# Weights' signs from ScalarE's parametric ReLU, and eight heads with split values in place of four

## The chip, the cores and the metric

The kernel runs on one core of a Trainium2 chip. The metric is the time of one execution on the device in microseconds (us), smaller is better; the time before is the median of three runs. A core has five engines that matter here: TensorE (PE in the profile; PEld is its weight load), VectorE (DVE), ScalarE (ACT), GpSimd (POOL) and SyncE (SP). Each runs its own instructions in the order in which they were queued, and waits for others by semaphores. POOL and SP here mostly start transfers between memory and the on-chip buffer.

## The reference

An attention in which a query sees only the keys in its own hash bucket (six sign bits of a projection), and then two feed-forward blocks without residuals:

```
mask   = q_bucket[:, :, :, None] == k_bucket[:, :, None, :]     # (2, 8, 768, 768)
scores = where(mask, q @ k.T / sqrt(64), -1e9)
x = softmax(scores) @ v                    # 16 heads; x is (1536, 512)
h = x @ w_in                               # 512 x 2048
x = (h * tanh(softplus(h))) @ w_out        # 2048 x 512
a = x @ w1;  b = x @ w2                    # 512 x 1024 each
out = ((a * b) @ w3) @ w_out2              # 1024 x 1024, 1024 x 512
```

The inputs q, k, v and proj are float32; the six weight matrices are float64 and reach the kernel as pairs of 32-bit words.

## The kernel before, in words

**Precision.** Most products run on PE in a fast reduced format (`FR` in the code, `fp32r` in the profile). Where that is not exact enough, a factor is split into a high part (a cast to `FR`) and a low part (the rest), and the product takes three or four fast passes. The other way is one product in full float32, which PE takes more slowly and which the profile shows as two instructions.

**Attention.** 16 heads, numbered u = 0 to 15, each of 768 rows in six tiles of 128. For each score tile: four matmuls on PE (L537), the row maximum on DVE (L546), the exponential on ACT (L549). Then each 128 x 128 piece of the exponentials is transposed on PE (L591, three to an operation), copied out of PSUM into a tile T by ACT or DVE (L415), and multiplied by the values: a head has six value steps, each over two blocks of keys (L620, function `values`). In most heads the value step is two float32 products with 64 columns each. In the heads of `FRV`, before u = 3 to 6, values are split: the copy casts T to `FR`, a DVE subtraction makes T's low part (L600), the values themselves are cast (`vh`, on ACT or DVE) and subtracted (`vl`, L449) once a head into one tile that holds both parts, and the step is four fast products with 128 columns. A Val of kind "v" in pool F4 holds the split values; its limit (`Val(F4, "v", 3, FR)`) says how many heads may have one at a time.

**Weights.** 36 chunks of 128 x 1024 float64 numbers are loaded by POOL (L668, 1 MB each) and turned into float32 by `decode`: ACT scales the high words, read as float32, so that their exponents fall where a shift by three bits makes them those of the result (step a, L652, a Copy with a scale); DVE shifts (step b, L655), puts in the low words' upper bits (step c, L658) and the sign bit of step a's result (step d, L661). Twelve chunks make the product w3 @ w_out2 during the first heads (L743 to L770). The other 24 are stored to memory, and loaded and split (L710 on ACT, L712 on DVE) when their matmuls come.

**Stages.** The 1536 rows are three blocks of 512. Block 0's feed-forward (L959, L975, L1070) is mixed with heads 8 to 15 on PE. Blocks 1 and 2 come after the attention, with products on quarter tiles that need seven multiplications for eight (L906, L1327, L1369).

**What sets the order.** Every operation is given to a planner, `Plan.op`, with the engines that may run it, a cost, and a due time; `Plan.run` lays them out engine by engine: at each turn it takes the engine that can start first, and of its ready operations the one due first. An operation with two engines (`EITHER`) goes to the one that can start it first. Buffers are given out in the same pass, and the instructions are then recorded in the order of planned starts. The numbers in `CFG` are due times (`prep`, `wp0`, `dec0`, `ff0`, `clk` and others) and buffer limits (`hl`, `F`), so a changed number or cost moves instructions all over the program. Gaps on PE in the first part are filled with products that nobody reads (L406).

Of the kernel before, what the change touches and what calls it, by code (L numbers as in the profile page):

```python
# [8 lines left out]
F32 = mybir.dt.float32  # L9
FR = mybir.dt.float32r  # L10
I32 = mybir.dt.int32
AF = mybir.ActivationFunctionType
ALU = mybir.AluOpType
# [6 lines left out]
LEAST = float(2.0 ** -126)  # L20
HUGE = float(2.0 ** 100)
TINY = float(2.0 ** -80)
SIGN = -(2 ** 31)

PASS = ((0, 0), (0, 1), (1, 0))

CFG = {
    "lag": 1.92,
    "prep": 11.76,
    "wp0": 16.6,  # L30
    "wp1": 42.29,
    "dec0": 39.06,
    "dec1": 124.72,
    "ff0": 55.14,
    "ff1": 118.67,
    "slack": 0.10,
    "k8": 12,
    "f4": 7,
    "hl": 3,
    "hl2": 6,  # L40
    "sl": 2,
    "lag2": 1,
    "lag3": 1,
    "hlk": 2,
    "ahead": 13.19,
    "clk": 190.46,
    "g2": 3,
    "F": 2,
    "cold": 8.0,
    "fill": 60.0,  # L50
    "tc": 0,
    "T": 8,
    "VP": 3,
    "fv0": 3,
    "fv1": 7,
}


# [36 lines left out]
class Plan:  # L95
# [87 lines left out]
    def run(self):  # L183
        todo = {e: [] for e in self.free}
        count = 0
        for u in self.pending:
            if u.left == 0:
                for e in u.alts:
                    todo[e].append(u)
        total = len(self.pending)  # L190
        self.pending = []
        order = []

        def grab_time(u):
            t = 0.0
            for v in u.vals:
                if v.pool is not None and v.slot is None:
                    p = v.pool
                    if p.kinds.get(v.kind, 0) >= v.lim or not p.free:
                        return None  # L200
                    t = max(t, min(p.free)[0])
            return t

        while count < total:
            best = None
            for e, cand in todo.items():
                s = None
                for u in cand:
                    if u.start is not None:
                        continue  # L210
                    t = max(u.ready, self.free[e])
                    if s is not None and t > s + 1e-9:
                        continue
                    g = grab_time(u)
                    if g is None:
                        continue
                    t = max(t, g)
                    if s is None or t < s:
                        s = t
                if s is not None and (best is None or s < best[0]):  # L220
                    best = (s, e)
            if best is None:
                left = [u for e in todo for u in todo[e] if u.start is None]
                raise RuntimeError("plan is stuck: " + ", ".join(f"{u.name}({u.due:.1f})" for u in left[:40]))
            s, e = best
            pick = None
            for u in todo[e]:
                if u.start is not None or max(u.ready, self.free[e]) > s + 1e-9:
                    continue
                if pick is not None and (u.due, u.idx) >= (pick.due, pick.idx):  # L230
                    continue
                g = grab_time(u)
                if g is None or g > s + 1e-9:
                    continue
                pick = u
            u = pick
            u.start, u.eng = s, e
            for v in u.vals:
                if v.pool is not None and v.slot is None:
                    p = v.pool  # L240
                    f = min(x for x in p.free)
                    p.free.remove(f)
                    v.slot = f[1]
                    v.since = s
                    p.kinds[v.kind] = p.kinds.get(v.kind, 0) + 1
            cost = u.alts[e] * (1.7 if e == "PE" and s < CFG["cold"] else 1.0)
            u.alts[e] = cost
            end = s + cost
            if u.grow:
                u.grow(end + 0.5)  # L250
            self.free[e] = end
            order.append(u)
            count += 1
            todo[e] = [x for x in todo[e] if x.start is None]
            for v in u.vals:
                if v.pool is not None and not v.pin and all(x.start is not None for x in v.users):
                    t = max(self.out_time(x, True, _ANY) for x in v.users)
                    v.pool.free.append((t, v.slot))
                    v.pool.spans.setdefault(v.slot, []).append((v.since, t))
                    v.pool.kinds[v.kind] -= 1  # L260
            for x, data in u.succ:
                x.ready = max(x.ready, self.out_time(u, data, x))
                x.left -= 1
                if x.left == 0:
                    for ee in x.alts:
                        todo[ee].append(x)
        order.sort(key=lambda u: (u.start, u.idx))
        if self.filler:
            self.fill(order)
            order.sort(key=lambda u: (u.start, u.idx))  # L270
        for u in order:
            u.fn(u.eng) if len(u.alts) > 1 else u.fn()
        return order
# [26 lines left out]
def kernel(  # L300
# [14 lines left out]
    nc = tc.nc  # L315
# [6 lines left out]
    NH = B * H  # L322
# [10 lines left out]
    P = Plan()  # L333
# [30 lines left out]
    F4 = anypool("f", CFG["f4"], 1024, const)  # L364
# [65 lines left out]
    def load_v(u, due, after=()):  # L430
# [11 lines left out]

        P.op("POOL", 1.3, total, r=[t], w=[m], due=u * C, name=f"vs{u}")
        if u in FRV:
            g = vs[u] = Val(F4, "v", 3, FR)
            gv = lambda: g()[:, 0:2 * C * D].rearrange("p (c s d) -> p c s d", c=C, s=2)
            P.op(EITHER, (act(C * D, True), dve2(C * D)), lambda e: copy(e, gv()[:, :, 0], t()), r=[t], w=[(g, "hi")],
                 due=u * C + 1, name=f"vh{u}")
            P.op("DVE", dve(C * D), lambda: nc.vector.tensor_sub(out=gv()[:, :, 1], in0=t(), in1=gv()[:, :, 0]),  # L449
                 r=[t, (g, "hi")], w=[(g, "lo")], due=u * C + 1.1, name=f"vl{u}")  # L450
# [74 lines left out]
    E, st, et, pv = {}, {}, {}, {}  # L525
    X = [Val(K8, "X", 3) for _ in range(NBK)]
    v_mvs, v_rd, v_mean = Val(), Val(), Val()
    FRV = range(CFG["fv0"], CFG["fv1"])

    def scores(u, i, due):  # L530
        qb, kb, qa, ka = feat[u]
# [118 lines left out]
    def decode(raw, g, due, nm):  # L650
        rv = lambda: raw().rearrange("p (n t) -> p n t", t=2)
        P.op("ACT", 1.04, lambda: nc.scalar.activation(  # L652
            out=g(), in_=rv()[:, :, 1].bitcast(F32), func=AF.Copy, scale=2.0 ** -112),
            r=[raw], w=[g], due=due, name=nm + "a")
        P.op("DVE", 0.605, lambda: nc.vector.tensor_scalar(  # L655
            out=rv()[:, :, 1], in0=g().bitcast(I32), scalar1=3, scalar2=None, op0=ALU.logical_shift_left),
            r=[g], w=[raw], due=due + 0.1, name=nm + "b")
        P.op("DVE", 1.137, lambda: nc.vector.scalar_tensor_tensor(  # L658
            out=rv()[:, :, 1], in0=rv()[:, :, 0], scalar=29, in1=rv()[:, :, 1],
            op0=ALU.logical_shift_right, op1=ALU.bitwise_or), r=[raw], w=[raw], due=due + 0.2, name=nm + "c")  # L660
        P.op("DVE", 1.137, lambda: nc.vector.scalar_tensor_tensor(  # L661
            out=g().bitcast(I32), in0=g().bitcast(I32), scalar=SIGN, in1=rv()[:, :, 1],
            op0=ALU.bitwise_and, op1=ALU.bitwise_or), r=[raw, g], w=[g], due=due + 0.3, name=nm + "d")

    def rawload(src, due, nm, after=()):
        raw = Val(K8, "raw", 2, I32)
# [783 lines left out]
```

## Time and profile before

| | |
|---|---|
| median of three runs | 793.85 us (792.96 to 794.03) |
| the profiled execution | 793.21 us |
| its span, first to last instruction | 791.4 us |
| granted TensorE clock | 1.00 in every stretch |
| busy: PE, DVE, ACT, POOL | 775.5, 641.7, 490.0, 85.3 us |

The profile is one execution, read in several views: busy time by engine over the whole span or a stretch of it, instructions grouped by line and shape, the timeline in order of start, and the chain of waits that ends with the last instruction. Matmuls are pipelined, so an instruction's duration on PE is longer than the time until the next one starts; in the timeline the difference of two starts is what an operation costs PE. The first score matmul of head 2 starts at 44.7 us, of head 4 at 96.6, of head 7 at 182.0, of head 11 at 277.0; the last of all at 428.3. From 505.0 us on, PE does nothing for block 0 any more.

### The profile page before, as it was taken

To read this page: it belongs to the slowest core of one execution; us is meant where nothing else is said; L and a number is where in the kernel's file an instruction comes from. 1 tells how busy PE (TensorE), PEld (TensorE's weight loads), DVE (VectorE), ACT (ScalarE), POOL (GpSimd) and SP (SyncE) were. 2 spreads that over 40 slices of the span, in tenths; PEclk is the share of its full clock that TensorE was granted. 3 is DMA by queue.
4 is the path that set the end of the run, shared out by engine and by line. 5 is a ranking of instruction groups with operands and counts; after the bars stand their busy time and mean duration, and the time that the engine had idled before them with its cause. 6 is when DMAs were issued, how large, how long until landed. Compare 5 with 4: busy or idle time off the path is not lost.

```text
span 791.4 us, 12290 instructions
## 1 busy us (share of the span) xinstructions
PE 775.5 (98%) x4594; PEld 637.4 (81%) x4594; DVE 641.7 (81%) x1020; ACT 490.0 (62%) x811; POOL 85.3 (11%) x154
## 2 busy tenths in 40 slices
PE   8999899999999999999999999999999999999998
PEld 7766788888677767777776688999999889999987
DVE  5999799999999998889899799875655975686741
ACT  4898556668799777786766554664655643444420
POOL 3112011021132121121211100000000000000000
PEclk9999999999999999999999999999999999999999
DMA  7664545477688676677625461411224410110011
GB/s 222 206 238 119 191 164 154 121 253 212 199 274 253 206 224 200 225 217 221 229 82 190 165 255 48 140 54 55 76 85 129 119 47 1 54 54 1 1 54 54
DMA packets 39220, 114.53 MB, mean 145 GB/s; under 512 B 4836, under 2 KB 11332, under 8 KB 38136
## 3 DMA queue, kind: packets, MB, share of 16 engines
q0 software_dynamic: 16256, 65.02, 23.7%
q1 hardware_dynamic: 22904, 48.72, 21.0%
q8 instruction: 36, 0.59, 0.3%
q14 instruction: 24, 0.20, 0.1%
HBM read 83.89 MB, written 17.87 MB: 129 GB/s over the span
## 4 chain that ended last, share of the span: by engine, by line
PE 83%; DVE 10%; ACT 4%; issue 2%; DMA 1%; ACTq 0%; DVEq 0%; SPq 0%
PE q L906 19%; PE b L1327 11%; PE b L975 7%; PE b L620 7%; PE s L537 6%; PE b L1070 6%; PE b L591 6%; PE b L1369 6%; PE b L760 5%; PE b L959 4%; DVE st L546 2%; PE s L481 2%; PE s L510 2%; PE b L406 1%; DMA v<-in_v_dram 1%
## 5 line engine op out<-in xcount | busy, mean ns | idle before, releaser
L906 PEld LDWEIGHTS q<-k,k 128*128 128x128 f32 x1344 | 163.5, 189 | 4.0 <-DVE f L934 1.2
L906 PE MATMUL q<-k,k 128*128 128x256 f32 x1344 | 164.7, 281 | 0.8 <-DVE f L934 0.8
L712 DVE TENSOR_TENSOR k<-f,k 128x1024 fp32r<-128x1024 f32 x92 | 111.6, 1223 | 12.8 <-ACT k L710 12.6
L710 ACT CAST k<-f 128x1024 fp32r<-128x1024 f32 x92 | 95.2, 1050 | 34.9 <-PE b L975 9.3
L549 ACT ACTIVATE E<-s,st 128x768 f32<-128x768 f32 x96 | 86.8, 904 | 30.6 <-DVE st L546 21.4
L934 DVE TENSOR_TENSOR f<-q,f 128x256 f32<-128x256 f32 x128 | 51.6, 421 | 59.4 <-ACT f L939 39.6
L546 DVE TENSOR_REDUCE st<-s 128x1 f32<-128x768 f32 x96 | 90.9, 950 | 4.8 <-PE s L537 4.1
L591 PE MATMUL b<-ident,E 128*128 128x128 f32 x576 | 91.8, 274 | 1.6 <-ACT T L415 0.6
L591 PEld LDWEIGHTS b<-ident,E 128*128 128x128 f32 x576 | 71.4, 140 | 24.1 <-issue 3.0
L1327 PE MATMUL b<-k,k 128*128 128x512 f32 x384 | 90.6, 391 | 0.0
L1327 PEld LDWEIGHTS b<-k,k 128*128 128x128 f32 x384 | 71.1, 188 | 14.4
L975 PE MATMUL b<-k,k 128*128 128x512 f32 x288 | 77.6, 405 | 0.8 <-DVE k L640 0.8
L975 PEld LDWEIGHTS b<-k,k 128*128 128x128 f32 x288 | 51.2, 188 | 19.0 <-issue 8.4
L939 ACT COPY f<-q 128x256 f32<-128x256 f32 x64 | 23.8, 371 | 68.7 <-PE q L906 66.2
L620 PE MATMUL b<-T,v 128*64 128x384 f32 x288 | 63.1, 511 | 0.0
L537 PE MATMUL s<-kb,qb 128*128 128x384 f32 x192 | 55.6, 370 | 1.7 <-ACT E L549 1.0
L959 PE MATMUL b<-k,k 128*128 128x512 f32 x192 | 55.8, 413 | 0.0
L415 ACT COPY T<-b 128x384 f32<-128x384 f32 x91 | 41.9, 479 | 20.5 <-PE b L591 19.2
L760 PE MATMUL b<-k,k 128*128 128x512 f32 x192 | 51.5, 402 | 2.9 <-ACT T L415 2.5
L537 PE MATMUL s<-ka,qa 76*128 76x384 f32 x192 | 49.6, 339 | 0.0
L1070 PE MATMUL b<-k,k 128*128 128x512 f32 x192 | 49.0, 400 | 0.5 <-ACT T L415 0.5
L1369 PE MATMUL b<-k,f 128*128 128x512 f32 (+1 forms) x216 | 47.1, 368 | 0.0
(132 smaller groups left out, 1210.3 us busy)
## 6 DMA issues: line engine op xcount, KB each, us to landing
k<-in_moe_w_dram POOLq DMA_DIRECT2D x16, 1024.0 KB, 7.3
k<-in_moe_w_out_dram POOLq DMA_DIRECT2D x12, 1024.0 KB, 6.4
k<-in_moe_w_in_dram POOLq DMA_DIRECT2D x8, 1024.0 KB, 6.5
f<-keep_wo SPq DMA_DIRECT2D x16, 512.0 KB, 3.3
keep_wi<-f POOLq DMA_DIRECT2D x8, 512.0 KB, 5.5
f<-keep_wi POOLq DMA_DIRECT2D x8, 512.0 KB, 4.9
keep_wo<-f POOLq DMA_DIRECT2D x8, 512.0 KB, 4.3
f<-keep_wo POOLq DMA_DIRECT2D x8, 512.0 KB, 7.6
```

The lines of the kernel that those rows point to most:

```text
L537: nc.tensor.matmul(t()[:, a, 0:HS], lhsT=l()[0:kk, i * 128:(i + 1) * 128], rhs=r()[0:kk, a * HS:(a + 1) * HS], start=(l is qb), stop=(l is ...
L546: P.op("DVE", 0.868, lambda: nc.vector.tensor_reduce(out=s()[:, 0, i:i + 1], in_=t()[:, :, 0:HS], axis=AX.XY, op=ALU.max, negate=True), r= ...
L591: nc.tensor.transpose(t()[:, ci * 128:(ci + 1) * 128], es[ci]()[:, kt * 128:(kt + 1) * 128], ident)
L620: nc.tensor.matmul(t()[r, 0:HS], lhsT=w, rhs=f(), start=first and j == 0, stop=last and j == CH - 1)
L710: P.op("ACT", act(1024, True), lambda: nc.scalar.copy(out=hl()[:, 0:1024], in_=f()), r=[f], w=[(hl, 0)], due=due, name="hi")
L712: P.op("DVE", dve(1024), lambda: nc.vector.tensor_sub(out=hl()[:, 1024:2048], in0=f(), in1=hl()[:, 0:1024]), r=[f, (hl, 0)], w=[(hl, 1)], ...
L760: nc.tensor.matmul(acc(), lhsT=hv()[:, ws, g_, :], rhs=wview(wo2[g_ // 2], 2)[:, rs, g_ % 2, :], start=(n == 0), stop=(n == 3 * GT - 1))
L906: nc.tensor.matmul(q()[:, c * NH_:(c + 1) * NH_], lhsT=lhs(w, i), rhs=xs[i][x]()[:, qcol(o)], start=first and n == 0, stop=n == 5, skip_gr ...
L975: nc.tensor.matmul(of(), lhsT=l(), rhs=rr(), start=(m == 0), stop=(m == len(ops) - 1))
L1070: nc.tensor.matmul(t(), lhsT=wview(w, KD)[:, ws, kk, f2 * 128:f2 * 128 + 128], rhs=kview(x2[kk // 2], xs, kk), start=(kk == 0 and s == 0), ...
L1327: nc.tensor.matmul(t(), lhsT=wview(w, 2)[:, ws, f, dd * 128:(dd + 1) * 128], rhs=gv[:, gs, f, :], start=(j == 0 and f == 0 and s == 0), st ...
L1369: nc.tensor.matmul(t()[:, c], lhsT=gv[:, gs, t4 * 128:(t4 + 1) * 128], rhs=wview(w, 2)[:, ws, f % 2, c], start=(f == 0 and s == 0), stop=( ...
```

## The change

In `decode` step a becomes a parametric ReLU with the slope -(2 ** 32) for negative inputs. A positive number is scaled as before. A negative one comes out positive and 2 ** 32 times as large, which sets one more bit of its exponent field; step b's shift moves that bit into the sign's place. So step d is gone, and step c writes the result. The set of heads with split values becomes a bit mask, 31800: heads 3, 4, 5 and 10 to 14. The limit on tiles of split values goes from 3 to 1. In the planner DVE is offered an `EITHER` operation 0.14 later than ACT, and the numbers in `CFG` are others:

```diff
 CFG = {
...
-    "dec0": 39.06,
-    "dec1": 124.72,
+    "dec0": 59.2,
+    "dec1": 140.06,
...
-    "hl": 3,
+    "hl": 4,
...
-    "clk": 190.46,
+    "clk": 118.97,
+    "pen": 0.14,
+    "vl": 1,
+    "fm": 31800,
...
-    "F": 2,
+    "F": 3,
...
-    "fv0": 3,
-    "fv1": 7,
...
-                    t = max(u.ready, self.free[e])
+                    t = max(u.ready + (CFG["pen"] if len(u.alts) > 1 and e == "DVE" else 0.0), self.free[e])
...
-            g = vs[u] = Val(F4, "v", 3, FR)
+            g = vs[u] = Val(F4, "v", CFG["vl"], FR)
...
-    FRV = range(CFG["fv0"], CFG["fv1"])
+    FRV = [x for x in range(NH) if CFG["fm"] >> x & 1]
...
         P.op("ACT", 1.04, lambda: nc.scalar.activation(
-            out=g(), in_=rv()[:, :, 1].bitcast(F32), func=AF.Copy, scale=2.0 ** -112),
+            out=g(), in_=rv()[:, :, 1].bitcast(F32), func=AF.Prelu, scale=2.0 ** -112, alpha=-(2.0 ** 32)),
             r=[raw], w=[g], due=due, name=nm + "a")
...
         P.op("DVE", 1.137, lambda: nc.vector.scalar_tensor_tensor(
-            out=rv()[:, :, 1], in0=rv()[:, :, 0], scalar=29, in1=rv()[:, :, 1],
-            op0=ALU.logical_shift_right, op1=ALU.bitwise_or), r=[raw], w=[raw], due=due + 0.2, name=nm + "c")
-        P.op("DVE", 1.137, lambda: nc.vector.scalar_tensor_tensor(
-            out=g().bitcast(I32), in0=g().bitcast(I32), scalar=SIGN, in1=rv()[:, :, 1],
-            op0=ALU.bitwise_and, op1=ALU.bitwise_or), r=[raw, g], w=[g], due=due + 0.3, name=nm + "d")
+            out=g().bitcast(I32), in0=rv()[:, :, 0], scalar=29, in1=rv()[:, :, 1],
+            op0=ALU.logical_shift_right, op1=ALU.bitwise_or), r=[raw], w=[g], due=due + 0.2, name=nm + "c")
```

How the order moves is shown at three places. The numbers behind names tell buffers of one kind apart. Behind `decode` lines of after stand two or three lower than those of before; above it they stand one higher.

DVE, at the end of head 2, before: two decodes (b, c, d are L655, L658, L661), with the score maxima and the split of the product's transposes between.

```order
L655 TENSOR_SCALAR k_604<-f_716 128x1024
L751 TENSOR_TENSOR k_722<-b_67,k_722 128x512
L658 SCALAR_TENSOR_TENSOR k_604<-k_604 128x1024
L640 TENSOR_TENSOR k_448<-b_70,tm_104 64x128
L661 SCALAR_TENSOR_TENSOR f_716<-f_716,k_604 128x1024
L640 TENSOR_TENSOR k_519<-b_70,tm_104 64x256
L751 TENSOR_TENSOR k_722<-b_67,k_722 128x512
L546 TENSOR_REDUCE st_111<-s_74 128x1
L712 TENSOR_TENSOR k_765<-f_716,k_765 128x1024
L655 TENSOR_SCALAR k_614<-f_735 128x1024
```

DVE at the same place of the changed kernel (L656 and L659 are b and c).

```order
L656 TENSOR_SCALAR k_602<-f_723 128x1024
L450 TENSOR_TENSOR f_690<-v_100,f_690 128x6x64
L659 SCALAR_TENSOR_TENSOR f_723<-k_602 128x1024
L547 TENSOR_REDUCE st_111<-s_75 128x1
L416 CAST hlqk_98<-rw_96 128x6x64
L656 TENSOR_SCALAR k_617<-f_732 128x1024
L416 COPY T_779<-b_69 128x384
L473 TENSOR_TENSOR hlqk_98<-rw_96,hlqk_98 128x6x64
```

A decode is two DVE operations instead of three, and copies of T and the next head's splits have moved in between.

ACT in head 3, before: the cast of head 5's values (`f_894<-v_100`) between the third and fourth exponential (`E_81`, `E_82`) of head 3.

```order
L415 COPY T_868<-b_69 128x384
L415 COPY T_878<-b_70 128x384
L549 ACTIVATE E_81,st_109<-s_75,st_109 128x768
L415 CAST f_894<-v_100 128x6x64
L748 CAST k_862<-b_67 128x512
L415 COPY T_904<-b_70 128x384
L549 ACTIVATE E_82,st_109<-s_74,st_109 128x768
```

ACT in the changed kernel: the cast of head 5's values (`f_1485<-v_100`) stands behind the fourth exponential of head 5 itself.

```order
L550 ACTIVATE E_82,st_111<-s_74,st_111 128x768
L653 ACTIVATE f_1468<-k_1079 128x1024
L746 CAST k_1452<-b_67 128x512
L416 CAST f_1485<-v_100 128x6x64
L416 CAST T_1488<-b_68 128x384
L628 COPY tm_104<-b_70 64x384
```

The cast moved two heads back in ACT's queue; in SP's queue the load of head 5's values stands at number 36 of 209, where it was number 42.

DVE in head 12, before: values are not split there, and two decodes stand between the maxima.

```order
L655 TENSOR_SCALAR k_3258<-f_3388 128x1024
L546 TENSOR_REDUCE st_110<-s_74 128x1
L658 SCALAR_TENSOR_TENSOR k_3258<-k_3258 128x1024
L661 SCALAR_TENSOR_TENSOR f_3388<-f_3388,k_3258 128x1024
L640 TENSOR_TENSOR k_519<-b_67,tm_103 64x256
L640 TENSOR_TENSOR k_2335<-b_67,tm_103 64x128
L415 COPY T_3466<-b_69 128x384
L712 TENSOR_TENSOR k_3451<-f_3247,k_3451 128x1024
L546 TENSOR_REDUCE st_110<-s_75 128x1
```

DVE in head 12 of the changed kernel: every T tile has its subtraction (L601).

```order
L656 TENSOR_SCALAR k_3235<-f_3376 128x1024
L601 TENSOR_TENSOR T_3490<-b_67,T_3481 128x384
L416 CAST T_3492<-b_69 128x384
L1033 TENSOR_TENSOR k_2590<-b_70,k_2590 128x512
L601 TENSOR_TENSOR T_3504<-b_69,T_3492 128x384
L547 TENSOR_REDUCE st_110<-s_74 128x1
L641 TENSOR_TENSOR k_528<-b_68,tm_103 64x256
L641 TENSOR_TENSOR k_2336<-b_68,tm_103 64x128
L601 TENSOR_TENSOR T_3525<-b_67,T_3511 128x384
L659 SCALAR_TENSOR_TENSOR f_3376<-k_3235 128x1024
```

Two subtractions and a cast stand between a decode's steps b and c where there was one maximum. Over heads 11 to 15 the order has 56 such subtractions (none before), 9 decodes (12 before) and 23 copies out of PSUM on DVE (33 before).

## Rows read from the trace of the kernel before

**Rows 1.** The page's busy time, us (share of the span) and instructions, by engine.

```profile
PE 775.5 (98%) x4594; PEld 637.4 (81%) x4594; DVE 641.7 (81%) x1020; ACT 490.0 (62%) x811; POOL 85.3 (11%) x154
```

**Rows 2.** Stretches: length, busy PE, PEld, DVE, ACT, POOL; clock, DMA share, GB/s.

```profile
44.70:96.60 51.90, 47.02 (x277) 34.40 (x275) 47.52 (x68) 38.57 (x77) 7.54 (x12) 1.00 0.58 195
96.60:182.00 85.40, 83.91 (x501) 73.84 (x500) 82.15 (x139) 54.39 (x105) 12.73 (x21) 1.00 0.58 181
277.00:428.30 151.30, 149.93 (x794) 108.00 (x792) 138.71 (x199) 111.56 (x177) 29.63 (x49) 1.00 0.64 202
505.00:788.10 283.10, 282.86 (x1866) 259.38 (x1866) 177.74 (x303) 133.13 (x198) 0.00 (x0) 1.00 0.18 58
```

**Rows 3.** Chain of waits: start, us, what; heads 2, 3 and later.

```profile
48.17 0.96 DVE st L546
...
56.41 1.13 DVE k L658
...
74.53 8.65 DMA v<-in_v_dram
...
84.64 4.38 PE b L760 x18
...
187.33 0.93 DVE T L600 x2
```

**Rows 4.** Timeline: start, us, engine, line, what, count [idle before <-who].

```profile
73.53 1.61 POOL L668 DMA_DIRECT2D k<-in_moe_w_dram  x3
...
74.53 0.33 SPq L433 DMA_DIRECT2D v<-in_v_dram  x1
...
83.20 0.51 ACT L415 CAST f<-v 128x384 fp32r<-128x384 f32 x1 [3.98 <-DMA v<-in_v_dram]
...
84.64 4.38 PE L760 MATMUL b<-k,k 128*128 128x512 f32 x18 [2.49 <-ACT T L415]
```

**Rows 5.** Timeline of PE alone, head 11: an unsplit step and score matmuls.

```profile
303.43 0.52 PE L537 MATMUL s<-ka,qa 76*128 76x384 f32 x2
303.88 0.87 PE L620 MATMUL b<-T,v 128*64 128x384 f32 x4
304.68 0.71 PE L481 MATMUL s<-identr,hlqk 128*128 128x128 f32 x6
...
310.52 0.52 PE L537 MATMUL s<-ka,qa 76*128 76x384 f32 x2
310.88 0.86 PE L975 MATMUL b<-k,k 128*128 128x512 f32 x3
```

**Rows 6.** Timeline of PE alone, head 2: transposes ahead of an unsplit step.

```profile
58.67 0.49 PE L591 MATMUL b<-ident,E 128*128 128x128 f32 x3
59.09 0.87 PE L620 MATMUL b<-T,v 128*64 128x384 f32 x4
```

**Rows 7.** Timeline of PE alone, 126 to 133 us: two split steps.

```profile
126.81 0.88 PE L620 MATMUL b<-T,f 128*128 128x384 f32 x4
127.53 2.23 PE L760 MATMUL b<-k,k 128*128 128x512 f32 x9
...
131.82 0.49 PE L591 MATMUL b<-ident,E 128*128 128x128 f32 x3
132.07 0.93 PE L620 MATMUL b<-T,f 128*128 128x384 f32 x4
132.84 0.38 PE L591 MATMUL b<-ident,E 128*128 128x128 f32 x2
```

**Rows 8.** Groups by line: count | busy us, mean ns | idle before <-who.

```profile
L661 DVE SCALAR_TENSOR_TENSOR f<-f,k 128x1024 int32<-128x1024 int32 x36 | 43.9, 1219 | 0.4
...
L652 ACT ACTIVATE f<-k 128x1024 f32<-128x1024 f32 x36 | 41.8, 1160 | 0.0
...
L1304 ACT ACTIVATE f<-f 128x1024 f32<-128x1024 f32 x16 | 17.0, 1061 | 4.5 <-DVE f L934 4.5
```

**Rows 9.** Stretches, the sign operation (L661) alone: length, DVE busy (count).

```profile
44.70:96.60 51.90, 7.31 (x6) 1.00 0.58 195
277.00:428.30 151.30, 14.62 (x12) 1.00 0.64 202
```

More of the change, by code (lines that the diff above doesn't have):

```diff
@@ L22 @@
 TINY = float(2.0 ** -80)
-SIGN = -(2 ** 31)
 PASS = ((0, 0), (0, 1), (1, 0))
 CFG = {
[L28 to L31, printed above, removed]
-    "dec0": 39.06,
-    "dec1": 124.72,
-    "ff0": 55.14,
-    "ff1": 118.67,
+    "lag": 1.91,
+    "prep": 10.83,
+    "wp0": 15.86,
+    "wp1": 43.49,
+    "dec0": 59.2,
+    "dec1": 140.06,
+    "ff0": 53.74,
+    "ff1": 118.96,
     "slack": 0.10,
@@ L44 @@
     "hlk": 2,
-    "ahead": 13.19,
-    "clk": 190.46,
+    "ahead": 10.68,
+    "clk": 118.97,
+    "pen": 0.14,
+    "vl": 1,
+    "fm": 31800,
     "g2": 3,
-    "F": 2,
+    "F": 3,
     "cold": 8.0,
@@ L227, in run @@
             for u in todo[e]:
-                if u.start is not None or max(u.ready, self.free[e]) > s + 1e-9:
+                r = u.ready + (CFG["pen"] if len(u.alts) > 1 and e == "DVE" else 0.0)
+                if u.start is not None or max(r, self.free[e]) > s + 1e-9:
                     continue
```

## The prediction

> **What bounds the kernel now.** I began with the page's busy shares [rows 1]: PE 98%, DVE 81% of a 791.4 us span. Averages over stages hide which engine sets the pace, so the table by stretches came next [rows 2]. I cut it where the first score matmul of a head starts: heads 2 and 3, heads 4 to 6, heads 11 to 15, and the tail after the last work on block 0. The reader is to see two things there. In the tail PE is busy 282.86 of 283.10 us and DVE only 177.74: nothing but PE work counts in it, and the change takes no PE work out of it. In heads 2 and 3, PE is idle for 51.90 - 47.02 = 4.9 us; in heads 4 to 6 for 1.5 us; in heads 11 to 15 for 1.4 us. So PE sets the pace nearly everywhere, DVE is close behind it up to the tail, and heads 2 and 3 are the one place past the start where PE waits for something worth having.
>
> What PE waits for there is in the chain of waits [rows 3]: from 48 to 74 us it runs through DVE (score maxima, decode steps at 1.13 us each back to back), then through one load of values that lasts 8.65 us, and PE starts again at 84.64. The timeline of that spot [rows 4] says why a load of 192 KB is on the path: ScalarE's queue holds the cast of head 5's values two heads early, the load was issued at 74.53 beside weight loads of 1 MB each, and ScalarE sat 3.98 us in front of that cast. PE then waited 2.49 us for a copy that stood behind it.
>
> **The change part by part.** The sum is made against the profiled execution, 793.21 us (span 791.4 and 1.8 around it); the median of the three runs is 793.85, 0.6 above, which is less than their spread of 1.1, so I carry no correction.
>
> *PE: four more heads have split values.* Each head has six value steps. An unsplit step takes two float32 products; from its start to the next instruction's start it is 0.80 us (303.88 to 304.68) [rows 5]. It also delays itself: the score matmuls ahead of it take 0.45 us where the same pair ahead of something else takes 0.36 (310.52 to 310.88) [rows 5], and three transposes ahead of it take 0.42 us [rows 6] against 0.25 ahead of a split step (131.82 to 132.07) [rows 7]. So 0.89 to 0.97 us. A split step has four products at 0.72 to 0.77 us [rows 7]. The middle difference is 0.93 - 0.75 = 0.18 us; 4 heads x 6 steps x 0.18 = **4.3 us** less PE work; the bounds are 24 x 0.12 = 2.9 and 24 x 0.25 = 6.0. PE is the bound, so this lies on the path.
>
> *DVE: the sign operation leaves, split values come.* 36 decodes lose an operation of 1.22 us, 1.13 us back to back [rows 3, 8]: 40.7 us out. In come 48 subtractions of the transposed weights' low parts, 0.47 us each back to back (0.93 us for two) [rows 3, 8], and four of the values': 24.4 us. The order puts eight evacuations of 256 or 512 columns, and a feature copy, on ScalarE instead: some 4 us, most of it in the tail. The number of copies out of the transposes on DVE is 69 in both. Net about -20 us of 641.7. What that is worth depends on where:
>
> Heads 2 and 3: six sign operations stood here [rows 9], 6.8 us of 51.9, in the very stretch where the chain is DVE's; the order has five decodes there now instead of six and no split value until the last steps of head 3. DVE work falls from 47.5 to some 40 us, and PE's own 47.0 us becomes the bound. The early cast goes too: with one split tile allowed instead of three, head 5's cast stands at head 5's fourth score, two heads later, while its load stands earlier in SP's queue than before. Its wait of 3.98 us has nothing left to wait for. Of the 4.9 us of PE idle I take **3.9 us** back and leave 1.0 for the latency that heads 4 to 6 show (1.5 us in three heads). Bounds: 0 (the waits come back behind another late load) and 4.9.
>
> Heads 11 to 15: here DVE gets worse. By the order, 56 subtractions and four of values come in (60 x 0.47 = 28.2 us); 12 sign operations [rows 9] and three decodes' other two steps, 1.13 and some 0.6, go (13.6 + 5.2), and ten copies (4.7). DVE 138.7 + 4.7 = 143.4 us. PE loses 29 steps x 0.18 and six 512-column matmuls that the order moves ahead: 151.3 - 5.2 - 1.4 = 144.7 us. The two engines come level. In heads 4 to 6, where all values were split already, DVE was busy 82.15 of 85.40 us and PE idle for only 1.5 [rows 2]: split values do work beside a DVE at 96%. I charge **+1.2 us** for being level (bounds 0 and the slower rival below).
>
> *ScalarE: Prelu for Copy.* The trace has no Prelu. A Copy of 1024 columns takes 1.16 us here and Mish on 1024 columns 1.06 [rows 8]: the function does not show in the price, so I take 0 difference; the other end is a second pass, 36 x 1.06 = 38 us. The order has 18 table loads before and after, so Prelu brings none. ScalarE is busy 38.57 of 51.90 and 54.39 of 85.40 us [rows 2]; even the dear end fits in there and would delay decodes that have several us of cover. Cost nothing; without that cover it would be felt in heads 2, 6 and 9, where four decodes stand together: some 4 us.
>
> *The order.* The second stage's rows come a little earlier (12 matmuls of it stand among block 0's last output matmuls), the amount of PE work is the same, and DVE's preparation for it stands well ahead in both. The wait at that seam is under 1 us. Value loads, feature copies and weight loads keep their numbers; a new collision of loads like that at 74.53 can't be read from an order, which is why the bound of the second term is 0. Nothing for the forecast.
>
> Sum: 793.2 - 4.3 - 3.9 + 1.2 = **786.2 us**.
>
> **The rivals.** *DVE's relief counts in full.* If DVE sets the pace up to the tail, its 20 us come off the time: 793.2 - 20 = 773. For it: DVE is busy 92 to 96% in the three stretches ahead of the tail [rows 2]. Against it: PE's starts follow each other without a gap in [rows 5, 7], and its idle time is 791.4 - 775.5 = 15.9 us in all, start and end among it; with 4.3 us of less work, 20 us would take every gap that there is. The Trainium skill speaks for this rival: its page "Perfetto Trace Analysis", section "Identifying the Most-Contended Engine", calls the matmuls' busy share a poor measure of headroom and wants that of weight loads instead, which is 71% in heads 11 to 15 (108.00 of 151.30) and 92% in the tail. By that rule PE has room and DVE is the engine to relieve. The row-by-row starts contradict it for this mix of 512-column matmuls and float32 products, so it gets little.
>
> *DVE becomes the bound in heads 11 to 15, with the idle share it has there now.* It is busy 138.71 of 151.30 us there, 91.7%, and in heads 2 and 3, where the chain was its own, no more than 47.52 of 51.90, 91.6% [rows 2]. If it can't be fuller, the stretch takes 143.4 / 0.916 = 156.6 us where I count on 144.7 + 1.4 + 1.2 = 147.3: 9.3 us more, 795.5. It decides from a share of 93%: at 143.4 / 0.93 = 154.2 us the 7 us of gain are gone. For it: a split step needs transpose, cast, subtraction and product in turn, and 1.13 us decode steps stand between in DVE's one queue. Against it: heads 4 to 6 ran so at 96%.
>
> *Gain given back.* PE work falls, but heads 2 and 3 keep their waits (another late load) and the level engines cost 3 us more: 793.2 - 4.3 + 4.2 = 793.
>
> *The change does not do what it says* (Prelu dearer by a pass): 786.2 + 4 = 790, inside the forecast's range.
>
> **How the numbers follow.** Forecast 786.2, its own range 781 to 791: chance 0.66. Full relief, about 773: 0.08. Given back, 791 to 795: 0.17, half of it under 792.3. DVE the bound, about 795.5: 0.09. The range has to reach 8 in 10. Below, both terms at their good bounds and the 2.9 us of idle in heads 4 to 6 and 11 to 15 gone would be 793.2 - 6.0 - 4.9 - 2.9 = 779.4: from 779. Above, it goes to 792.5, through the nearer half of the third case; outside lie the two far cases and the other half. This kernel's measurement can tell 0.2%, 1.6 us, from no change: faster means under 792.3, 0.66 + 0.08 + 0.08 = 0.82; same 0.09; slower 0.09.
>
> **What would show it.** Right, if PE's idle time in heads 2 and 3 is near 1 us and no wait of some us for a value load stands in ScalarE's queue; if the sign line is gone from DVE and the Prelu line stays near 1.16 us; if heads 11 to 15 take 145 to 148 us with DVE over 96% busy; if the tail keeps 283 us within 1. Wrong in the second term, if PE waits 4 us or more between 45 and 97 us; wrong in the third, if PE's waits for DVE's low parts add up to more than 3 us in heads 11 to 15; wrong as a whole, if the time up to the last score falls by far more than 8 us, which would say that DVE was the bound.

## The result, and the profile after

The changed kernel takes 780.89 us (median; 779.82 to 781.57), against 793.40 (792.72 to 794.03) for the kernel before on the same chip: a ratio of 0.984, 95% interval 0.982 to 0.986. The profiled execution of it has a span of 779.6 us, 11.8 less than before. The forecast was 786.2 with a range of 779 to 792.5: inside, but 5.3 us too high.

The page's busy time, by engine, of the changed kernel, to set against [rows 1]:

```profile
PE 767.6 (98%) x4594; PEld 649.7 (83%) x4594; DVE 619.1 (79%) x1028; ACT 495.4 (64%) x823; POOL 84.2 (11%) x154
```

PE has the same 4594 instructions and 7.9 us less busy time; DVE is 22.6 us lighter (the forecast said about 20). Span less busy is PE's idle time: 12.0 us, from 15.9.

The table by stretches of the changed kernel (length, then busy PE, PEld, DVE, ACT and POOL; clock, DMA share, GB/s), cut where heads 2, 4, 7 and 11 start and where the last score starts, and from the last work on block 0; to set against [rows 2]:

```profile
45.20:92.30 47.10, 45.63 (x278) 34.32 (x277) 41.38 (x65) 34.82 (x67) 5.72 (x11) 1.00 0.58 192
92.30:173.70 81.40, 80.96 (x488) 70.91 (x487) 70.68 (x125) 55.30 (x108) 14.18 (x22) 1.00 0.56 174
173.70:272.80 99.10, 98.17 (x559) 70.02 (x557) 88.95 (x142) 80.53 (x139) 20.58 (x34) 1.00 0.77 245
272.80:416.80 144.00, 141.42 (x788) 122.82 (x785) 140.99 (x233) 111.46 (x187) 25.61 (x44) 1.00 0.55 176
...
492.50:776.40 283.90, 283.64 (x1868) 259.46 (x1866) 172.26 (x295) 137.21 (x208) 0.00 (x0) 1.00 0.18 59
```

Heads 7 to 10 have no row among those of before; this is it:

```profile
182.00:277.00 95.00, 93.85 (x540) 69.43 (x538) 91.64 (x144) 82.19 (x146) 19.10 (x33) 1.00 0.72 225
```

Heads 4 to 6 lose 13 matmuls and heads 7 to 10 gain 19, so these two are read together. Beside each stage stands what the prediction's terms make of it: its 29 steps and six matmuls in heads 11 to 15, so that 2.3 us of its 4.3 for PE come back earlier (six matmuls more, and head 6 unsplit).

| stage | before | after | difference | by the prediction |
|---|---|---|---|---|
| up to head 2 | 44.7 | 45.2 | +0.5 | 0 |
| heads 2 and 3 | 51.9 | 47.1 | -4.8 | -3.9 |
| heads 4 to 10 | 180.4 | 180.5 | +0.1 | +2.3 |
| heads 11 to 15 | 151.3 | 144.0 | -7.3 | -5.4 |
| after the last score | 363.1 | 362.8 | -0.3 | 0 |
| sum | 791.4 | 779.6 | -11.8 | -7.0 |

PE's waits in the changed kernel, by what it waited for (us in total, times, longest): first in heads 2 and 3, then in heads 11 to 15.

```profile
PE b L621 <- ACT T L416: 1.1, 1, 1.1
PE s L538 <- ACT E L550: 0.3, 1, 0.3
```

```profile
PE b L1068 <- DVE T L601: 1.6, 1, 1.6
PE b L973 <- DVE k L1033: 0.7, 2, 0.4
```

The stall of [rows 4] is gone. In heads 11 to 15, where DVE is now busy 140.99 of 144.00 us (97.9%), PE waits only 2.3 us for it.

Groups by line of the changed kernel (count | busy us, mean ns of one | idle before): the new low parts, step c and the Prelu. To set against [rows 8].

```profile
L601 DVE TENSOR_TENSOR T<-b,T 128x384 fp32r<-128x384 f32 x96 | 51.9, 547 | 4.4 <-ACT T L416 4.0
...
L659 DVE SCALAR_TENSOR_TENSOR f<-k 128x1024 int32<-128x1024 int32 x36 | 43.8, 1218 | 0.4
L653 ACT ACTIVATE f<-k 128x1024 f32<-128x1024 f32 x36 | 41.2, 1154 | 0.0
```

A Prelu takes 1154 ns where the Copy took 1160. And the timeline of PE alone in head 12 (start, duration, what), a place where nothing was split before; the step starts at 310.43 and the next instruction at 311.14, so it costs 0.71 us, as in [rows 7]:

```profile
310.07 0.52 PE L538 MATMUL s<-ka,qa 76*128 76x384 f32 x2
310.43 0.88 PE L621 MATMUL b<-T,f 128*128 128x384 f32 x4
311.14 0.49 PE L592 MATMUL b<-ident,E 128*128 128x128 f32 x3
```

### The profile page after: what moved, and what is told of

The parts are those of the page before. It is cut to its first block, busy times and chain, and to the rows that moved or that the text cites. A ratio compares the mean times of both kernels' runs of the same rounds, so it can differ in the third digit from the quotient of the medians.

```text
span 779.6 us, 12307 instructions
## 1 busy us (share of the span) xinstructions
PE 767.6 (98%) x4594; PEld 649.7 (83%) x4594; DVE 619.1 (79%) x1028; ACT 495.4 (64%) x823; POOL 84.2 (11%) x154
## 4 chain that ended last, share of the span: by engine, by line
PE 80%; DVE 12%; DMA 3%; issue 2%; ACT 2%; POOL 0%; SPq 0%; DVEq 0%; POOLq 0%; ACTq 0%
PE q L904 20%; PE b L1325 11%; PE b L621 6%; PE b L1068 6%; PE b L1367 6%; PE b L973 6%; PE s L538 5%; PE b L592 5%; PE b L758 4%; PE b L957 4%; DVE st L547 2%; DVE T L601 2%; PE s L511 2%; DMA k<-in_moe_w_out_dram 2%; DVE k L710 1%
## 5 line engine op out<-in xcount | busy, mean ns | idle before, releaser
L973 PEld LDWEIGHTS b<-k,k 128*128 128x128 f32 x288 | 52.0, 188 | 11.8 <-DVE k L1033 1.3
L601 DVE TENSOR_TENSOR T<-b,T 128x384 fp32r<-128x384 f32 x96 | 51.9, 547 | 4.4 <-ACT T L416 4.0
L416 ACT CAST T<-b 128x384 fp32r<-128x384 f32 x64 | 30.5, 481 | 24.5 <-PE b L592 22.0
```

What stands on the lines that cost most here:

```text
L973: nc.tensor.matmul(of(), lhsT=l(), rhs=rr(), start=(m == 0), stop=(m == len(ops) - 1))
```

## The experiments

The change has three parts (a shorter decode, eight heads, other numbers), and each has its own effect on PE, on DVE and on the order. "Old numbers" are the `CFG` of before; "planned anew" means that the planner laid out the whole program again. Each median is compared with the kernel before on its own chip (793.4 to 794.0).

| kernel | us | ratio [95%] |
|---|---|---|
| shorter decode in the old order | 788.82 | 0.994 [0.992, 0.995] |
| shorter decode, planned anew | 785.99 | 0.990 [0.988, 0.991] |
| limit of one tile, alone | 801.66 | 1.009 [1.008, 1.011] |
| eight heads, alone | 823.06 | 1.037 [1.035, 1.038] |
| after, with four heads | 790.84 | 0.997 [0.995, 0.998] |
| after, step c issued twice | 813.25 | 1.025 [1.023, 1.026] |
| shorter decode and eight heads, old numbers | 814.12 | 1.025 [1.021, 1.029] |
| shorter decode, no split head | 789.55 | 0.995 [0.993, 0.996] |
| the same with eight heads and one tile | 788.47 | 0.993 [0.991, 0.994] |
| and with the limits `hl` 4, `F` 3 | 792.15 | 0.997 [0.996, 0.999] |
| after, with two tiles | 800.41 | 1.008 [1.006, 1.009] |
| after, with nine heads | 788.68 | 0.993 [0.992, 0.995] |

Nine of these twelve medians lie outside the ranges of every side that was written down before the run; inside are only the rival of "shorter decode and eight heads, old numbers" and the theories of "no split head" and "eight heads and one tile". The causes below are therefore read from the stages of each run, not from a forecast that came true.

### What DVE's relief is worth

**The shorter decode in the old order.** Step d keeps its place and cost in the plan, but issues nothing. Every other instruction stands where it stood, so that 36 DVE operations are the whole difference; the output is the same.

```diff
-            ... func=AF.Copy, scale=2.0 ** -112),
+            ... func=AF.Prelu, scale=2.0 ** -112, alpha=-(2.0 ** 32)),
...
-            out=rv()[:, :, 1], in0=rv()[:, :, 0], scalar=29, ...
+            out=g().bitcast(I32), in0=rv()[:, :, 0], scalar=29, ...
...
-        P.op("DVE", 1.137, lambda: nc.vector.scalar_tensor_tensor(...), ... name=nm + "d")
+        P.op("DVE", 1.137, lambda: None, ... name=nm + "d")
```

> The kernel before with the parametric ReLU in step a and step c writing the result; the planner still plans step d, but nothing is issued for it. So every engine's order is that of before, and 36 DVE operations of 1.13 us are missing. Theory (PE sets the pace, DVE only in heads 2 and 3): of 40.7 us of DVE work only what stood on the chain in heads 2 and 3 comes back, minus what the wait for head 5's values keeps: 790 to 792.5 us, PE idle in heads 2 and 3 still above 2.5 us. Rival (DVE sets the pace up to the tail): some 15 us less, 778 or below. Rival (the gain is all in the new order): 793.

788.82 us, 5.2 less. Its stretches, cut at the same heads (2 to 3, 4 to 6, 7 to 10, 11 to 15):

```profile
44.50:94.40 49.90, 46.08 (x276) 34.18 (x275) 40.96 (x62) 38.01 (x77) 6.40 (x12) 1.00 0.60 203
94.40:179.20 84.80, 83.67 (x500) 73.88 (x499) 74.47 (x132) 54.56 (x104) 13.27 (x21) 1.00 0.58 182
...
179.20:273.10 93.90, 93.34 (x541) 69.63 (x539) 84.26 (x136) 82.19 (x146) 17.93 (x32) 1.00 0.73 228
...
273.10:424.30 151.20, 149.83 (x793) 107.93 (x791) 126.50 (x186) 110.89 (x177) 29.62 (x49) 1.00 0.63 202
```

36 x 1.13 = 40.7 us of DVE work (its busy time falls by 37.1) are worth 5.2. Of the 4.2 us between the two profiled spans, heads 2 and 3 give 2.0, heads 4 to 10 give 1.7 (180.4 to 178.7), and heads 11 to 15, where DVE's busy time falls by 12.2 us, give 0.1. DVE was not what bound that last stretch. There is a second thing to see. With the same PE instructions in the same order, PE's busy time fell from 775.5 to 773.4 us: short waits hide in what the profile models as busy, and idle time alone understates what a wait costs. The fall is not spread over all matmuls: 26 places among the 4594, at each of which the busy time up to PE's next start changed by more than 0.04 us, make up 2.0 of the 2.1 us.

**The shorter decode, planned anew.** Steps b and c as in the change, old numbers, old four heads.

> The kernel before with the three-step decode, planned anew, all numbers and the four split heads as before. Theory: 789 to 792 us; the planner uses the free DVE time for copies, but PE's work is unchanged. Rival (DVE sets the pace): under 783. Rival (the gain needs the new numbers or the split heads): 792 to 794.

785.99 us: the planner makes another 2.8 of the freed time, 8.0 in all, where the whole change gains 12.5. Heads 2 and 3, heads 4 to 6 and heads 11 to 15:

```profile
44.40:90.40 46.00, 45.72 (x277) 34.64 (x276) 42.77 (x68) 35.61 (x69) 8.81 (x13) 1.00 0.70 242
90.40:175.10 84.70, 83.61 (x501) 74.00 (x500) 75.95 (x135) 53.30 (x103) 11.60 (x20) 1.00 0.55 171
...
270.20:419.90 149.70, 149.67 (x793) 107.63 (x792) 128.42 (x196) 106.07 (x165) 28.29 (x47) 1.00 0.61 193
```

Heads 2 and 3 fall by 5.9 us and PE is idle 0.3 us there: the whole gain of that stage and more comes without the new numbers. The limit for split values is still 3. ScalarE's waits for transfers, in the old order of the experiment before and in this one (us in total, times, longest):

```profile
ACT f L415 <- DMA v<-in_v_dram: 4.8, 2, 2.4
ACT hlqk L415 <- DMA rw<-in_k_dram: 1.4, 1, 1.4
```

```profile
ACT hlqk L415 <- DMA rw<-in_k_dram: 1.4, 1, 1.4
```

The late value load went with the new plan, at the old limit. The lower limit is thus not needed for that; whether it is enough by itself is seen further down.

**After, with step c issued twice.** The mirror of the first: the same 40.7 us put back into DVE in the changed kernel's order (the second writes the same result).

```diff
+            for _ in range(2):
                 nc.vector.scalar_tensor_tensor(
                     out=g().bitcast(I32), in0=rv()[:, :, 0], scalar=29, in1=rv()[:, :, 1],
```

> The changed kernel, every engine's order as changed, but step c is issued twice (the second writes the same again): 36 DVE operations of 1.13 us that the planner knows nothing of, the load of the old sign operation. In the old order these cost 5 us. Theory (DVE is at 98% in heads 11 to 15 now and sets the pace there): the 9 there cost their full 1.13 us, 10 us, with some 3 more in heads 2 and 3 and behind the last score: 793 to 797. Rival (DVE's work is as hidden as in the old order): 785 to 787.

813.25 us, 32.4 above the changed kernel: 80% of the added work shows. Heads 2 and 3, 7 to 10 and 11 to 15:

```profile
47.20:100.50 53.30, 48.24 (x278) 35.22 (x277) 48.91 (x72) 35.27 (x68) 6.91 (x11) 0.97 0.53 169
...
184.40:290.60 106.20, 99.07 (x558) 69.87 (x556) 98.68 (x151) 80.87 (x138) 21.84 (x35) 1.00 0.70 224
290.60:447.20 156.60, 145.51 (x787) 121.85 (x785) 153.61 (x245) 111.16 (x186) 26.24 (x43) 1.00 0.50 162
```

In heads 11 to 15 DVE stays 98.1% busy and the stretch grows by 12.6 us for 12.6 us more of DVE's busy time. So the changed kernel has no DVE time left there, where the kernel before gave back nothing for 12.2 us less. The forecast had 10 us there and 3 elsewhere; elsewhere it was 19.4, with 6.2 in heads 2 and 3 and 7.1 in heads 7 to 10, where DVE had been busy only 88 and 90% of the time. An order that was planned without these operations pays for them also where DVE is not full. That the lighter DVE made room for the split values fits this, but is not shown by it: eight heads and one tile, planned with the four-step decode, were not run.

### What the eight heads are worth, and to whom

**The shorter decode, no split head.** The second experiment with `FRV = []`: 24 value steps back to float32 products.

> The kernel before with the three-step decode and no split head at all, numbers as before. Against the same with four split heads (786.0 us) PE does 24 unsplit steps more at 0.18 us, and DVE has 50 operations less. Theory (PE sets the pace): 786 + 4.3 = 790. Rival (DVE sets the pace): 786 or less, by up to 20 us.

789.55 us, 3.6 more. Heads 4 to 6:

```profile
90.60:177.80 87.20, 87.20 (x503) 64.54 (x501) 62.36 (x101) 50.43 (x96) 11.96 (x22) 1.00 0.57 176
```

PE is busy for the whole of it, 3.6 us more than with split values, for 18 steps: 0.20 us a step, or 0.17 if the two matmuls more in this cut are taken off at 0.24. Over the span PE's busy time is 779.3 us against 774.1: 5.2 / 24 = 0.22. That is too much by what a low clock adds in this run, in one place in heads 7 to 10:

```profile
222.90:226.30 3.40, 3.40 (x11) 2.93 (x11) 3.40 (x6) 2.42 (x6) 1.37 (x3) 0.50 0.88 307
```

By estimate 3.4 us at half the clock hold 1.7 us of work, so that (5.2 - 1.7) / 24 = 0.15 us is the lower end. The step's price in the prediction, 0.18 (0.12 to 0.25), holds.

**Eight heads alone**, with the four-step decode and the old numbers:

```diff
-    FRV = range(CFG["fv0"], CFG["fv1"])
+    FRV = [x for x in range(NH) if 31800 >> x & 1]
```

> The kernel before with split values in heads 3, 4, 5 and 10 to 14, decode with the sign operation, planned anew. DVE work rises by some 24 us. Theory: PE's work falls by 4.3 us, but DVE in heads 11 to 15 (138.7 of 151.3 us busy before) gets 28 us more minus the copies that go to ScalarE, and becomes the bound there: 793 to 800 us. Rival (PE bound holds, DVE's load does not matter): 789.

823.06 us, 29 more. Heads 11 to 15, then from the last score to the second stage's start:

```profile
284.20:428.00 143.80, 136.52 (x755) 116.48 (x753) 140.59 (x224) 104.62 (x171) 25.81 (x41) 1.00 0.47 157
428.00:526.60 98.60, 81.74 (x345) 61.58 (x344) 89.98 (x135) 46.18 (x62) 13.93 (x22) 0.91 0.58 206
```

Heads 11 to 15 are as short as in the changed kernel, but with 39 matmuls fewer than before in them; these come after the last score, and PE is idle 16.9 us there. The longest wait, from the timeline of PE (in brackets: idle before, and whom for):

```profile
463.25 19.29 PE L1070 MATMUL b<-k,k 128*128 128x512 f32 x72 [9.88 <-ACT k L710]
```

**Shorter decode and eight heads, old numbers.** Does the lighter DVE carry the eight heads by itself?

> The kernel before with the three-step decode and the eight split heads, but all numbers as before (due times, limits, three tiles of split values). Theory (the decode makes the room that the heads need): 786 - 4.3 = 782 us. Rival (the heads need the new due times, else block 0's weights are ready too late, as with eight heads and the old decode): 790 or more, with waits of PE for L710 or L712 behind the last score.

814.12 us; the theory's 782 falls, the rival holds. The profiled execution took 808.5 us. Its heads 11 to 15, then up to the second stage:

```profile
272.00:396.50 124.50, 116.22 (x659) 100.59 (x658) 113.85 (x195) 88.27 (x158) 17.69 (x30) 0.99 0.42 126
396.50:510.10 113.60, 102.18 (x441) 79.05 (x441) 95.83 (x139) 61.77 (x82) 16.90 (x27) 0.95 0.61 212
```

The last score comes 20 us earlier than in the changed kernel, with 788 - 659 = 129 matmuls fewer in heads 11 to 15, at a DMA share of 0.42: block 0's weights are fetched late, and PE later waits 10.2 us for their splits (L707 on ScalarE, L709 on DVE). What delays them was a guess here: up to three tiles of split values now live in heads 10 to 14, in the pool of seven buffers (F4) that the fetched weights use too.

**The same with one tile** tests that guess:

```diff
-            g = vs[u] = Val(F4, "v", 3, FR)
+            g = vs[u] = Val(F4, "v", 1, FR)
```

> The kernel with the three-step decode, eight split heads and the old numbers (814.1 us), with one tile of split values at a time instead of three. Theory (in heads 10 to 14 three tiles of split values hold three of the seven F4 buffers that block 0's weights and sums are loaded and made in, so these come late): the wait behind the last score goes, the last score is later than 396 us and the stretch behind it shorter than 407; 783 to 792 us. Rival (the due times of decodes and fetches are the cause): 805 to 815.

788.47 us: 25.7 us come back with this one number. Heads 7 to 10 and 11 to 15 of the profiled execution, which took 791.44 us, and PE's longest wait (it is in head 7):

```profile
175.30:279.00 103.70, 97.94 (x539) 68.70 (x537) 90.03 (x143) 81.47 (x139) 21.95 (x36) 0.97 0.77 251
279.00:425.10 146.10, 143.02 (x790) 123.45 (x789) 142.76 (x235) 109.65 (x180) 27.05 (x45) 1.00 0.55 177
```

```profile
192.26 1.54 PE L620 MATMUL b<-T,v 128*64 128x384 f32 x2 [4.54 <-DVE T L415]
```

Behind this wait stands a load. The chain of waits has it until 190.92 us (start, duration, what), DVE waits 6.3 us in front of the operation that needs it, and the copy of T comes after that in DVE's queue:

```profile
177.84 13.08 DMA f<-r_d
```

In the changed kernel DVE's wait for such a load is shorter:

```profile
DVE f L795 <- DMA f<-r_d: 1.3, 1, 1.3
```

**After, with two tiles** (`"vl": 2`) asks the same from the other side.

> The changed kernel with two tiles of split values at a time instead of one, planned anew. Theory of the buffers: a second tile takes one of seven F4 buffers from block 0 in heads 10 to 14: 783 to 795 us. Rival (one tile makes the next head's first value step wait, two relieve it): under 780.

800.41 us: one tile more costs 19.5. Heads 11 to 15, then up to the second stage:

```profile
276.30:415.30 139.00, 135.91 (x760) 118.10 (x759) 135.97 (x226) 106.76 (x175) 21.40 (x38) 1.00 0.51 157
415.30:497.20 81.90, 72.51 (x307) 53.54 (x307) 66.97 (x103) 44.54 (x65) 12.13 (x20) 0.94 0.60 219
```

28 matmuls slip past the last score, and PE is idle 9.4 us behind it. Both sides agree that the tiles are what holds block 0's work back. That it happens through F4 is the code's reason; a trace shows no buffers.

**The limit of one tile, alone**, in the kernel before:

> The kernel before with one tile of split values allowed instead of three, planned anew. Theory: the cast of head 5's values is late, ScalarE's wait of 3.98 us for its load is gone, PE idle in heads 2 and 3 falls by some 2.5 us: 790.5 to 792 us. Rival (the stall was only covered by DVE's chain, or another load is late in its place): 793 to 795.

801.66 us, 7.6 more. The late value load is gone, and heads 2 and 3 take 49.1 us, 2.8 less; but heads 7 to 10 take 3.2 more, and behind the last score PE is idle 4.5 us:

```profile
179.80:278.00 98.20, 94.37 (x539) 69.11 (x538) 89.10 (x139) 79.39 (x143) 18.81 (x30) 1.00 0.62 186
429.40:503.50 74.10, 69.60 (x305) 51.87 (x305) 67.27 (x103) 37.65 (x52) 9.69 (x16) 0.98 0.58 199
```

So the limit by itself is enough to take the late load away, and still no gain: it loses more behind heads 2 and 3. It is what the eight heads need.

**After, with four heads** (`"fm": 120`, heads 3 to 6):

> The changed kernel with the old four split heads (3 to 6), all else as changed, planned anew. Against it the changed kernel has four more heads split. Theory (a split step is 0.18 us cheaper on PE and DVE has the room that the sign operations left): 781 + 4.3 = 785 us, PE's busy time some 4 to 5 us above that of the changed kernel. Rival (the gain beyond the decode is in the new numbers, not in the heads): 781 or less.

790.84 us, 10.0 more than with eight, and PE's busy time is 8.1 us above that of the changed kernel, where 4 to 5 were expected. Heads 7 to 10 and 11 to 15:

```profile
172.80:276.40 103.60, 99.20 (x555) 71.97 (x554) 93.23 (x148) 83.65 (x144) 20.94 (x36) 1.00 0.73 230
276.40:425.30 148.90, 148.69 (x790) 106.84 (x789) 127.09 (x192) 112.01 (x178) 29.78 (x50) 1.00 0.66 211
```

Heads 11 to 15 take 4.9 us more than in the changed kernel, heads 7 to 10 another 4.5, and there PE is idle for 4.4 us instead of 0.9. So the 10.0 us are not the price of the steps alone: 24 at 0.20 are 4.8. With the same four heads and decode the old numbers gave 786.0. So the new numbers, the limit of one tile among them, cost 4.9 us at four heads; at eight heads they gain 7.6 (788.47 with the limit already at 1, to 780.89). The two are not alike: the limit is in the first and not in the second, and alone it cost 7.6 us in the kernel before.

**The other limits**, `hl` 4 and `F` 3, on top of eight heads and one tile:

> As the run before, and the two other limits of the changed kernel with it: four high-low weight tiles instead of three (hl), three PSUM banks for block 0 instead of two (F). Due times and the offer to DVE stay old. Theory (limits make the changed kernel's gain, due times only trim it): 780 to 785 us. Rival (due times): 795 or more.

792.15 us, with a spread from 788.25 to 793.9: no gain, and a miss. DVE's wait for `f<-r_d` in head 7 is here too, 6.4 us. The 7.6 us must be in the due times and DVE's 0.14, or in these together with the limits; that is inferred from what is left, and no run here takes them one by one. The trace says where a part of it lies: the profiled executions of eight heads with one tile and of the changed kernel are 10.0 us apart, and 4.6 of these are in heads 7 to 10 (103.7 against 99.1), the place of that late load.

**Nine heads** (`"fm": 31864`, head 6 added) asks whether there is more to be had:

> The changed kernel with head 6 split as well (nine heads), planned anew. In heads 4 to 6 DVE is at 87%, so there is room there. Theory (a split step saves PE some 0.2 us where DVE has room): 1 us less, 779.5 to 780.5. Rival (every added DVE operation counts at some 0.8 of its length, as the repeated step c showed): 13 operations of 0.47 us more, 781 + 5 - 1 = 785.

788.68 us, 7.8 more than with eight, and beyond what either side expected. Heads 7 to 10, then behind the last score:

```profile
173.40:275.30 101.90, 98.74 (x556) 72.71 (x554) 92.02 (x148) 84.05 (x145) 22.70 (x36) 1.00 0.74 235
...
419.20:485.30 66.10, 63.45 (x279) 47.47 (x278) 59.42 (x96) 36.62 (x52) 8.53 (x14) 0.97 0.65 229
```

Six steps at 0.2 would be 1.2 us less PE work. Instead PE's idle time over the span grows by 4.6 us (16.6 against 12.0), and its busy time by 2.7 (770.3 against 767.6). No version faster than the changed kernel was found. The changed kernel's own numbers with the four-step decode, and with three tiles, were not tried.

## Why the prediction was near, step by step

**The eight heads (-4.3): the price holds, that it comes off the time depends on the order.** The run without split heads gives 0.15 to 0.22 us a step, 3.5 to 5.2 us for 24. From the shorter decode with four heads (786.0) to the changed kernel (780.9) the time falls by 5.1, but the limit and the other numbers change there too. With old numbers and one tile the eight heads cost 2.5 us (786.0 to 788.5), with the new numbers they gain 10.0 (790.8 to 780.9). "PE is the bound, so this lies on the path" thus held in the new order and not in the old one. In heads 11 to 15 PE's busy time fell by 149.93 - 141.42 = 8.5 us; six matmuls are 1.4 of it and 29 steps at 0.20 are 5.8. The last 1.3 us are not explained.

**Heads 2 and 3 (-3.9): 4.8, and both reasons hold.** PE's idle time fell from 4.88 to 1.47 us, as foreseen; 1.4 us more came out of its busy time, where short waits hide. DVE's relief alone gives 2.0 us there in the old order and 5.9 planned anew. The limit of one tile alone takes the late load away and gives 2.8 there. Each of the two is enough to move that load, and which of them did it in the changed kernel is not shown. What the prediction did not see is that the limit alone costs more elsewhere (801.66 us in all).

**DVE's relief elsewhere (0): the step that failed.** "Net about -20 us of 641.7. What that is worth depends on where": it was then given a value in heads 2 and 3 alone, 3.9 us with the late load in it. The shorter decode planned anew gains 8.0 us by itself. For heads 4 to 10 the terms leave +2.3 us and the trace has +0.1; the shorter decode gave 1.7 us there in the old order and 0.6 planned anew, so that how much of this is DVE's relief is argued and not shown. I read PE's 1.5 us of idle time in heads 4 to 6 as all that DVE cost it. The last score comes 11.5 us earlier (428.3 to 416.8) where the sum had 7.0; heads 4 to 10 are 2.2 of the 4.5 us between, heads 11 to 15 are 1.9 and heads 2 and 3 are 0.9, less 0.5 ahead of them. The text meant to doubt itself beyond 8 us and to call DVE the bound then; that reading does not hold for heads 11 to 15, where the relief alone gave 0.1 us.

**Level engines (+1.2): right in size.** PE's idle time in heads 11 to 15 rose from 1.4 to 2.6 us, by 1.2, with DVE at 97.9%. The text's "147.3" for the stretch counted the old 1.4 us of idle time twice; by its own terms it is 151.3 - 5.2 - 1.4 + 1.2 = 145.9, and 144.0 was measured, below the 145 to 148 that it announced. By the same correction the second rival's price is 10.7 us (156.6 - 145.9) and not 9.3.

**Prelu (0): right.** 1154 ns against 1160. **After the last score:** 362.8 us against 363.1, and from the last work on block 0 283.90 against 283.10, as foreseen.

**The order (0 "for the forecast"): right by luck.** The changed kernel as a whole keeps it near zero, but the same eight heads and decode take 814, 788 or 781 us by the numbers alone. That is a spread of 33 us, more than four times the forecast gain, and no rival of mine had it.

**The rivals.** Full relief (773) falls: in the old order 40.7 us less DVE work brought 5.2. The Trainium skill's page "Perfetto Trace Analysis", section "Identifying the Most-Contended Engine", spoke for it, since it wants TensorE's headroom judged by the weight loads' busy share and by the share of peak arithmetic. The second was not worked out here. The first was 71% in heads 11 to 15 (107.93 of 151.20 us in the old order), and yet 12.2 us less DVE work left the stretch as long as it was; PE's busy share, 99%, told the truth there. DVE as the bound at a share of 91.7% (795.5) falls too, since DVE ran there at 97.9%; at 98% the doubled step c added to that stretch as much as DVE's busy time grew.

## What to carry to other kernels

Work taken from an engine that is not the bound buys only a part of itself (of 41 us here 5 in the old order and 8 planned anew), but it can be spent on work that shortens the bound; price the two together, and expect that the freed engine, once it is level, will charge nearly full price for whatever is added. Do not take the profile's idle time for all that a wait costs: compare the same instructions at the same place with the neighbour lighter. And where a planner sets the order, a buffer's limit can weigh more than the arithmetic that it serves, so ask of each new long-lived tile whose buffer it holds.

## What the hardware showed beyond that

A parametric ReLU with a slope of -(2 ** 32) costs ScalarE no more than a Copy with a scale, 1154 against 1160 ns for 128 x 1024. The granted clock was 1.00 in every stretch of the kernels before and after in which PE worked. In other kernels it fell for some us, and the length of a wait does not tell when. With eight heads alone it was 0.50 from 457.4 to 467.6 us; a wait of 9.88 us ended at 463.25. With no split head it was 0.50 from 222.9 to 226.3 us, and PE had been idle only 1.4 us of the 6.9 before. The kernel before kept 1.00 all through heads 2 and 3, with 4.9 us of idle time [rows 2]. Of the two levels, 1.2 and 2.4 GHz, 0.50 is the lower one. Its cost is seen in matmuls of 512 columns of eight heads alone (L1070 only: length, PE busy, clock, DMA share, GB/s): from start to start they take 0.43 us in the first stretch and 0.23 in the second, so that some of the loss there is slower matmuls on top of the waits.

```profile
446.50:450.30 3.80, 3.80 (x10) 0.50 0.95 357
469.00:472.80 3.80, 3.80 (x18) 1.00 0.09 33
```
